# Combined weights' stores issued later, their combination ended earlier, and weight slices loaded ahead in an attention kernel with two expert layers

## The chip, the cores and the metric

The kernel runs on one core of one Trainium2 chip. The metric is the device time of one execution in microseconds. The profile adds one execution with its span (first to last instruction) and a trace of every instruction.

## What is computed

The reference joins an attention between a sequence and a set of states with two feed-forward layers, all in float32:

```python
scores = scale * np.matmul(x, state.transpose(0, 1, 3, 2))   # x: 8 x 8 x 512 x 64, state: 8 x 8 x 32 x 64
a = softmax(scores);        xread = np.matmul(a, state)
scores2 = scale * np.matmul(state, x.transpose(0, 1, 3, 2))
a2 = softmax(scores2);      sread = np.matmul(a2, x)
y = np.concatenate([xread, sread], axis=2)      # -> 4352 tokens x 512
h = y @ w_in                                    # 512 -> 2048, weights moe_*
y = (np.maximum(h, 0.0) + alpha * np.minimum(h, 0.0)) @ w_out
h = y @ w_in2                                   # weights moe2_*
out = (h - np.tanh(h)) @ w_out2
```

## The kernel before

Every float32 matrix is split into a high and a low part of a format that TensorE multiplies fast, and a product is three matmuls (high x high, high x low, low x high). The tokens are worked in nine blocks: blocks 0 to 7 have 512 tokens each (the sequence's reads of one batch), and the states' block has the 256 reads of the states of all batches. The order is 0 to 6, then the states' block, then block 7. In the plan below, index 6 (`B - 2`) is block 6, index 7 (`B - 1`) is the states' block and index 8 (`B`) is block 7.

**First layer.** A block is 16 visits f. Visit f issues the hidden tile f (`emit_h`, line 628), ScalarE and VectorE make the activation g of it (`act_a`, lines 634 and 635; `act_b`, lines 639 and 640), and TensorE adds the output product of the tile two visits back (`emit_o`, line 656), so `emit_o` of the last two tiles of a block falls into the first two visits of the next. In blocks 1 to 7 the weights are projected ones (`pw`), loaded in quarters by `load_parts` (line 443). For the states' block the plain weights are used, a slice of 128 columns per visit (`WS[f]`, tile ws, 512 KB in two DMAs), loaded from a copy in device memory by `load_w_in` (line 459). The block's input is the reads of the states, which each batch's attention stores (`xs<-xw`, line 610) and which are loaded in block 6, visit 13 (`load_reads`, line 699, tile yl). `split_reads` splits them (lines 348 on ScalarE, 349 on VectorE): two of the four column parts in visit 14 of block 6, two in visit 15. Beside this each block prepares the attention of the next ones.

**Combination.** The second layer's weights are used in combined form (a seven-product scheme). The generator `combine` makes them for 2 matrices of 8 pieces. For a piece, two raw tiles (`c_raw`, 512 KB each) are loaded one piece ahead (lines 104 and 110), ScalarE and VectorE turn the 64-bit words into integers (`c_m`, `c_q`, lines 113 to 125), GpSimd adds and subtracts them (`c_q`, `c_s`, line 238 and on), and the inner `parts` makes the split: a ScalarE copy into a `c_o` tile (line 263), GpSimd's subtraction of it (line 265), and the stores to device memory (line 267), seven of 256 KB for a piece. `c_raw` has 4 buffers, `c_o` 3. `combining` runs the second half of one piece step by step with the first half of the next, 9 steps per piece and 144 in all. Before, two steps are taken in each visit from visit 1 of block 3 on, until they are used up.

**Order.** All is written in program order by hand (`tc.manual_schedule`). Work that goes with a visit is put into a plan by `at(block index, visit, place, ...)`, with the places early (after `emit_h`), gap and mid (after `act_a`), late (after `emit_o` and `act_b`) and end. All DMAs are issued by SyncE in that order; an instruction that waits holds up those behind it on its engine. When a tile's buffer is used again, the new writer waits for the last reader of the old tile.

After block 7's third visit `open_slots` frees the combination's tiles (and before, would finish what is left of it), and the second layer begins its loads of combined weights (`ch<-wc`, later `wp<-wc`).

Of the kernel before, what the change touches and what calls it, by code (L numbers as in the profile page):

```python
# [12 lines left out]
F32 = mybir.dt.float32  # L13
F32R = mybir.dt.float32r
# [8 lines left out]
P = 128  # L23
# [12 lines left out]
def attention_and_two_mlps(ctx, tc, x, state, w1_in, w1_out, alpha, w2_in, w2_out, out):  # L36
    nc = tc.nc
    B, H, S, D = x.shape
# [4 lines left out]
    NCC = DM // P  # L43
    NF = DFF // P
# [56 lines left out]
    def raw_words(r, layer, f, half):  # L101
        if half == 0:
            wi = w1_in if layer == 0 else w2_in
            nc.sync.dma_start(
                out=r.rearrange("p (c f) w -> p c (f w)", c=NCC),
                in_=wi[:, 2 * f * P:2 * (f + 1) * P].rearrange("(c p) w -> p c w", p=P),
            )
        else:
            wo = w1_out if layer == 0 else w2_out
            nc.sync.dma_start(out=r.rearrange("p e w -> p (e w)"), in_=wo[f * P:(f + 1) * P, :])  # L110

    def high_abs(m, r):
        nc.scalar.activation(m.bitcast(F32), r[:, :, 1].bitcast(F32), AF.Abs)

    def high_word(m):
        nc.vector.tensor_scalar(m.bitcast(F32), m.bitcast(F32), HIGH_MAX, HIGH_MIN,
                                op0=ALU.min, op1=ALU.max)
        nc.vector.tensor_scalar(m, m, 3, LOW30, op0=ALU.logical_shift_left, op1=ALU.bitwise_and)

    def sign_word(m, r):  # L120
        nc.vector.scalar_tensor_tensor(m, r[:, :, 1], SIGN_TOP, m,  # L121
                                       op0=ALU.bitwise_and, op1=ALU.bitwise_or)

    def low_word(q, r):
        nc.scalar.activation(q, r[:, :, 0].bitcast(U32), AF.Copy, scale=2.0**-29)
# [78 lines left out]
    NJ, HW = NF // 2, DM // 2  # L204
    wc_dram = [[dram.tile([7, 2, P, 2, HW], F32, name=f"wc{m}_{j}") for j in range(NJ // 2)] for m in range(2)]

    def combine(mat, j, take, ahead):

        def raw(m, jj):
            got = []  # L210
            for h in range(2):
                r, done = take("raw")
                raw_words(r, 1, jj + h * NJ, m)
                got.append((r, done))
            return got

        got = ahead.pop((mat, j), None)
        if got is None:
            got = raw(mat, j)
        m, m_done, q, q_done = [], [], [], []  # L220

        def a(h):
            t, done = take("m")
            m.append(t)
            m_done.append(done)
            high_abs(t, got[h][0])

        def b(h):
            high_word(m[h])
            sign_word(m[h], got[h][0])  # L230
            t, done = take("q")
            q.append(t)
            q_done.append(done)
            low_word(t, got[h][0])
            got[h][1]()

        def c(h):
            nc.gpsimd.tensor_tensor(q[h], m[h], q[h], op=ALU.add)  # L238
            m_done[h]()

        a(0)
        yield
        a(1)
        b(0)
        yield
        b(1)
        c(0)
        yield
        c(1)
        n = (mat, j + 1) if j + 1 < NJ else (mat + 1, 0)  # L250
        if n[0] < 2:
            ahead[n] = raw(*n)
        yield "words"
        u, v = (t.bitcast(F32) for t in q)
        s, s_done = take("s")
        one, two = slice(0, HW), slice(HW, DM)
        sub = partial(nc.gpsimd.tensor_tensor, op=ALU.subtract)

        def parts(src, places):
            n = src.shape[-1]  # L260
            o, done = take("o")
            o = o[:, :, :n]
            nc.scalar.copy(o[:, 0], src)  # L263
            yield
            sub(o[:, 1], src, o[:, 0].bitcast(F32))  # L265
            for k, i in enumerate(places):
                nc.sync.dma_start(out=wc_dram[mat][j // 2][i, j % 2], in_=o[:, :, k * HW:(k + 1) * HW].bitcast(F32))
            done()

        if mat == 0:  # L270
            nc.gpsimd.tensor_tensor(s[:, one], v[:, one], v[:, two], op=ALU.add)
            sub(v[:, one], u[:, one], v[:, one])
            yield from parts(u, (0, 5))
            sub(s[:, two], v[:, two], v[:, one])
            yield from parts(v, (4, 6))
            sub(u[:, two], u[:, two], s[:, two])
            yield from parts(s, (1, 2))
            yield from parts(u[:, two], (3,))
        else:
            sub(s[:, one], u[:, one], u[:, two])  # L280
            sub(u[:, one], v[:, one], u[:, one])
            yield from parts(v, (3, 5))
            sub(s[:, two], v[:, one], s[:, one])
            yield from parts(u, (4, 0))
            sub(v[:, two], v[:, two], s[:, two])
            yield from parts(s, (1, 2))
            yield from parts(v[:, two], (6,))
        s_done()
        for done in q_done:
            done()  # L290

    def combining(todo, take):

        ahead, last = {}, None
        for n in [*todo, None]:
            now = combine(*n, take, ahead) if n else None
            working = now is not None
            while working or last is not None:
                if working:
                    working = next(now) != "words"  # L300
                    yield
                if last is not None:
                    if next(last, "end") == "end":
                        last = None
                    yield
            last = now
# [48 lines left out]
    def lead(b):  # L355
        return b if b % 2 else (b - 1) % B
# [95 lines left out]
    WS, late_pools = {}, []  # L452

    def load_w_in(f):
        if f < NF:
            WS[f] = late_pools[0].tile([P, 2, NCC, P], F32R, tag="ws", name=f"ws{f}", bufs=5)
            col = slice(f % FQ * P, (f % FQ + 1) * P)
            for part in range(2):
                nc.sync.dma_start(out=WS[f][:, part].bitcast(F32), in_=wi_dram[f // FQ][part][:, :, col])
# [274 lines left out]
    def load_chunk(o, i):  # L734

        t = slots.get([P, 2, 2, HW], F32R, f"ch{o}_{i}")
        nc.sync.dma_start(out=t.bitcast(F32), in_=wc_dram[0][o][i].rearrange("j p h c -> p j h c"))
        CH[o, i] = t
# [11 lines left out]
    def load_pair(u):  # L750
        for k in range(2):
            for m in range(2):
                load_pair_part(u, k, m)
# [315 lines left out]
    def at(i, f, when, *todo):  # L1069
        plan.setdefault((i, f, when), []).extend(todo)  # L1070
# [28 lines left out]
    with tc.manual_schedule():  # L1099
# [40 lines left out]
        for b in range(2, B):  # L1140
            for g in range(NG):
                i, f = (0, 0) if b == 2 else (b - 2, 6 + 7 * g) if b == lead(b) else (b - 2, 1 + g)
# [48 lines left out]
        def take(what):  # L1191
            shape, dtype, bufs = dict(raw=([P, DM, 2], I32, 4), m=([P, DM], I32, 2), q=([P, DM], I32, 4),
                                      s=([P, DM], F32, 2), o=([P, 2, DM], F32R, 3))[what]
            return late_pools[0].tile(shape, dtype, tag=f"c_{what}", name=f"c_{what}", bufs=bufs), lambda: None

        combined = combining([(m, j) for m in range(2) for j in range(NJ)], take)
        at(3, 0, "late", open_late)
        for i in range(3, B):
            for f in range(1 if i == 3 else 0, NF):
                for when in ("mid", "late"):  # L1200
                    at(i, f, when, lambda: next(combined, None))
        for f in range(4):
            at(B - 2, NF - 4 + f, "late", partial(load_w_in, f))
        for f in range(NF):
            at(B - 1, f, "early", partial(load_w_in, f + 4))

        fill = Filler()

        def open_slots():
            for _ in combined:  # L1210
                pass
            late_pools[0].release()
            freed.append(tc.alloc_tile_pool(name="slots_a", bufs=1, side="right", reuse_waits="tile"))
            slots.add(freed[0], "a", 16)
            load_pair(0)
            for i in range(7):
                load_chunk(0, i)

        freed = []
        at(B, 2, "late", open_slots)  # L1220
        at(B, 6, "early", lambda: fill.start(prepare_pair(0, 0)))
        for f in range(6, NF):
# [7 lines left out]
        for i, f in visits:  # L1230
            blk, n = seq[i]
# [142 lines left out]
```

## Time and profile before

| | |
|---|---|
| median of 3 runs | 1455.9 us (1454.38 to 1461.07) |
| the profiled execution's own time | 1458.23 us |
| its span | 1456.4 us |
| mean granted clock of TensorE | 0.981 of full speed |
| TensorE's busy time | 1393.9 us, 96% of the span |
| VectorE, ScalarE, GpSimd busy | 974.2, 731.0, 536.1 us |

The busy time of TensorE is modelled from its pipelined matmuls, so an engine that is shown busy is not at its peak. A granted clock of 1.00 is 2.4 GHz, 0.5 would be 1.2 GHz, and a value between is a mean over a stretch in which both were granted. An idle time is put down to what ended it.

### The profile page before, as it was taken

The numbers are of one execution on the slowest core, as the hardware profiler recorded it, in microseconds if no ns is written. First come the engines' busy times: TensorE is split into PE (matmuls) and PEld (weight loads), VectorE is DVE, ScalarE is ACT, GpSimd is POOL, SyncE is SP. The second block draws the span as 40 slices with busy tenths as digits, with TensorE's granted clock in tenths as the row PEclk, the third lists the DMA queues.
The fourth block names the chain that finished last, engine by engine and source line by source line (L and its number), as shares of the span: only waits on it lengthen the run. The fifth ranks groups of instructions, "written<-read, shape, count | busy, mean of one in ns | idle before, by whom it ended". The sixth has DMA issues, their size and how long they took to land.

```text
span 1456.4 us, 22830 instructions
## 1 busy us (share of the span) xinstructions
PE 1393.9 (96%) x8142; PEld 1188.7 (82%) x8142; DVE 974.2 (67%) x1436; ACT 731.0 (50%) x1326; POOL 536.1 (37%) x414
## 2 busy tenths in 40 slices
PE   5779899899999999999999999999999999999998
PEld 3557677677777778779977888888879999999998
DVE  7889766556666777764345656565357798877774
ACT  4666554444565656554335545454354354444443
POOL 3645400000554554445002212122035676666652
PEclk8989999999999999999999999999999999999999
DMA  6447568996677777689737774644968733444421
GB/s 184 138 136 210 168 181 313 301 304 192 197 219 216 205 243 221 204 245 307 245 79 273 252 252 153 220 167 146 345 253 319 252 114 120 146 138 138 145 81 37
DMA packets 230946, 293.43 MB, mean 201 GB/s; under 512 B 58288, under 2 KB 134064, under 8 KB 229808
## 3 DMA queue, kind: packets, MB, share of 16 engines
q1 hardware_dynamic: 230832, 291.97, 62.1%
q8 instruction: 64, 1.05, 0.3%
q14 instruction: 50, 0.41, 0.1%
HBM read 169.22 MB, written 120.59 MB: 199 GB/s over the span
## 4 chain that ended last, share of the span: by engine, by line
PE 66%; DVE 9%; DMA 9%; issue 3%; ACT 3%; SPq 2%; POOL 2%; ACTq 0%; DVEq 0%; POOLq 0%
PE ps_m L1038 20%; PE ps_m L848 17%; PE acc L656 15%; PE ps_h L628 9%; PE ps_p L416 2%; DMA wp<-wc 2%; DMA gt<-g 2%; PE ps_m L922 2%; DVE ps_h L635 1%; DVE g L640 1%; DMA pw<-pw 1%; ACT g L639 1%; DMA wc<-c_o 1%; DMA c_raw<-in_moe_w_out 1%; DMA ch<-wc 1%
## 5 line engine op out<-in xcount | busy, mean ns | idle before, releaser
L656 PE MATMUL acc<-g,wo 128*128 128x512 f32 (+1 forms) x1728 | 409.7, 387 | 1.7 <-ACT g L639 1.6
L656 PEld LDWEIGHTS acc<-g,wo 128*128 128x128 f32 x1728 | 315.0, 192 | 73.8 <-issue 6.5
L1038 PE MATMUL ps_m<-wp,s 128*128 128x256 f32 x2856 | 343.4, 283 | 1.1 <-ACT e L1021 1.1
L1038 PEld LDWEIGHTS ps_m<-wp,s 128*128 128x128 f32 x2856 | 343.0, 192 | 1.5 <-ACT e L1021 1.5
L848 PE MATMUL ps_m<-x,ch 128*128 128x512 f32 x1344 | 306.5, 390 | 3.3 <-ACT c L854 2.6
L848 PEld LDWEIGHTS ps_m<-x,ch 128*128 128x128 f32 x1344 | 251.9, 188 | 57.4 <-ACT c L854 3.8
L983 DVE TENSOR_TENSOR s<-gt,s 128x512 fp32r<-128x512 f32 (+1 forms) x216 | 215.2, 1046 | 48.5 <-ACT s L999 47.4
L640 DVE SCALAR_TENSOR_TENSOR g<-ps_h,sign,g 128x512 fp32r<-128x512 f32 (+1 forms) x144 | 103.5, 718 | 158.5 <-ACT g L639 158.4
L639 ACT ACTIVATE g<-ps_h,sign 128x512 fp32r<-128x512 f32 (+1 forms) x144 | 95.6, 664 | 178.5 <-PE acc L656 126.3
L999 ACT CAST s<-gt 128x512 fp32r<-128x512 f32 (+1 forms) x216 | 119.9, 597 | 81.0 <-PE ps_m L1038 38.7
L628 PE MATMUL ps_h<-x,pw 128*128 128x512 f32 x600 | 156.5, 396 | 3.1 <-DVE g L640 1.5
L635 DVE SCALAR_TENSOR_TENSOR ps_h<-ps_h,sign,t 128x512 f32<-128x512 f32 (+1 forms) x144 | 104.4, 725 | 60.2 <-ACT t L634 59.3
L628 PEld LDWEIGHTS ps_h<-x,pw 128*128 128x128 f32 x600 | 109.7, 188 | 28.5 <-DVE g L640 2.1
L861 POOL TENSOR_TENSOR t<-c,t 128x512 f32<-128x512 f32 x32 | 45.2, 1413 | 230.8 <-ACT t L858 225.9
L238 POOL TENSOR_TENSOR c_q<-c_m,c_q 128x512 int32<-128x512 int32 x32 | 41.3, 1292 | 232.7 <-DVE c_m L121 212.9
L870 DVE TENSOR_TENSOR c<-ps_m,c 128x512 f32<-128x512 f32 x96 | 65.8, 689 | 84.4 <-PE ps_m L848 71.8
L634 ACT ACTIVATE t<-ps_h,slope 128x512 f32<-128x512 f32 (+1 forms) x144 | 95.9, 666 | 49.5 <-PE ps_h L628 49.2
L858 ACT ACTIVATE t<-c 128x512 f32<-128x512 f32 x96 | 60.5, 633 | 85.1 <-DVE c L870 75.7
L265 POOL TENSOR_TENSOR c_o<-c_q,c_o 128x512 fp32r<-128x512 f32 (+1 forms) x48 | 56.1, 1169 | 97.0 <-ACT c_o L263 97.0
L965 POOL TENSOR_TENSOR s<-gt,gt 128x512 f32<-128x512 f32 (+1 forms) x36 | 52.8, 1476 | 87.4 <-DMA gt<-g 87.2
L854 ACT COPY c<-ps_m 128x512 f32<-128x512 f32 x96 | 56.0, 587 | 51.7 <-PE ps_m L848 44.6
L168 POOL TENSOR_TENSOR cq<-cm,cq 128x512 int32<-128x512 int32 x32 | 42.6, 1330 | 96.0 <-DVE cm L121 67.0
(146 smaller groups left out, 1647.9 us busy)
## 6 DMA issues: line engine op xcount, KB each, us to landing
g<-t SPq DMA_DIRECT2D x128, 256.0 KB, 2.3
gt<-g SPq DMA_DIRECT2D x64, 512.0 KB, 4.9
wc<-c_o SPq DMA_DIRECT2D x112, 256.0 KB, 3.6
ch<-wc SPq DMA_DIRECT2D x56, 512.0 KB, 7.0
pw<-pw SPq DMA_DIRECT2D x104, 256.0 KB, 5.1
wp<-wc SPq DMA_DIRECT2D x28, 512.0 KB, 7.0
pw<-ph SPq DMA_DIRECT2D x40, 256.0 KB, 2.9
pw<-pl SPq DMA_DIRECT2D x40, 256.0 KB, 2.7
```

Of the source, the lines that this page charges most:

```text
L628: nc.tensor.matmul(ps[:, :n], lhsT=w[i], rhs=xt[:, j, :n], start=(k == 0 and m == 0), stop=(k == len(pairs) - 1 and m == 2))
L634: nc.scalar.mul(t, ph, slope[:, f:f + 1])
L635: nc.vector.scalar_tensor_tensor(ph, ph, sign[:, f:f + 1], t, op0=ALU.mult, op1=ALU.max)
L639: nc.scalar.mul(g[:, 0, :n], ph, sign[:, f:f + 1])
L640: nc.vector.scalar_tensor_tensor(g[:, 1, :n], ph, sign[:, f:f + 1], g[:, 0, :n].bitcast(F32), op0=ALU.mult, op1=ALU.subtract)
L656: nc.tensor.matmul(acc[t][:, :n], lhsT=w[i][:, t * P:(t + 1) * P], rhs=g[:, j, :n], start=(first and k == 0), stop=(last and k == 2))
L848: nc.tensor.matmul(b, lhsT=w[p][:, cc], rhs=XT[key, i][cc][:, q], start=(i not in GOES_ON and cc == k == 0), stop=(cc == 1 and k == 2), sk ...
L858: nc.scalar.activation(t, h, AF.Tanh)
L870: nc.vector.tensor_tensor(h, ps[j, i], h, op=ALU.add)
L983: nc.vector.tensor_tensor(made[k - 1][:, 1], src, made[k - 1][:, 0].bitcast(F32), op=ALU.subtract)
L999: nc.scalar.copy(made[k][:, 0], source(blk, i, jj))
L1038: nc.tensor.matmul(dst[:, t * HW:(t + 1) * HW], lhsT=s[:, p, r, t * P:(t + 1) * P], rhs=w[:, q], start=first, stop=(jj == NJ // 2 - 1 and ...
```

## The change

A store of a combined part is no longer issued where its subtraction is, but kept in a list with the number of the step, and a new `combine_step` issues it after the step whose number is higher by two. In blocks 3 to 6 a third step is taken at the end of every odd visit and of visits 0 and 8; none is planned in the states' block. What would be left at visit 9 of block 6 is done there (`drain`). The slices of the states' block's weights use 12 buffers instead of 5: the 5 of ws, then the 4 of c_raw and the 3 of c_o. Slices 0 to 4 are loaded in visits 2 to 6 of block 6, slices 5 to 11 in visits 9 to 15, and slices 12 to 15 in visits 2 to 5 of the states' block.

```diff
@@ combine, parts @@
             sub(o[:, 1], src, o[:, 0].bitcast(F32))
             for k, i in enumerate(places):
-                nc.sync.dma_start(out=wc_dram[mat][j // 2][i, j % 2], in_=o[:, :, k * HW:(k + 1) * HW].bitcast(F32))
+                kept.append((turns_of[0], wc_dram[mat][j // 2][i, j % 2], o[:, :, k * HW:(k + 1) * HW].bitcast(F32)))
             done()
@@ before combining @@
+    kept, turns_of = deque(), [0]
+
+    def combine_step(n=1):
+        for _ in range(n):
+            turns_of[0] += 1
+            next(combined, None)
+            while kept and kept[0][0] < turns_of[0] - 1:
+                _, o, t = kept.popleft()
+                nc.sync.dma_start(out=o, in_=t)
@@ load_w_in @@
         if f < NF:
-            WS[f] = late_pools[0].tile([P, 2, NCC, P], F32R, tag="ws", name=f"ws{f}", bufs=5)
+            k = f % 12
+            tag, bufs = ("ws", 5) if k < 5 else ("c_raw", 4) if k < 9 else ("c_o", 3)
+            WS[f] = late_pools[0].tile([P, 2, NCC, P], F32R, tag=tag, name=f"ws{f}", bufs=bufs)
@@ the plan @@
         combined = combining([(m, j) for m in range(2) for j in range(NJ)], take)
+        def drain():
+            while next(combined, "end") != "end":
+                pass
+            while kept:
+                _, o, t = kept.popleft()
+                nc.sync.dma_start(out=o, in_=t)
+
         at(3, 0, "late", open_late)
-        for i in range(3, B):
+        for i in range(3, B - 1):
             for f in range(1 if i == 3 else 0, NF):
                 for when in ("mid", "late"):
-                    at(i, f, when, lambda: next(combined, None))
-        for f in range(4):
-            at(B - 2, NF - 4 + f, "late", partial(load_w_in, f))
-        for f in range(NF):
-            at(B - 1, f, "early", partial(load_w_in, f + 4))
+                    at(i, f, when, combine_step)
+                if f % 2 or f % 8 == 0:
+                    at(i, f, "end", combine_step)
+        for f in range(5):
+            at(B - 2, 2 + f, "late", partial(load_w_in, f))
+        at(B - 2, 9, "end", drain)
+        for f in range(5, 12):
+            at(B - 2, 4 + f, "early", partial(load_w_in, f))
+        for f in range(NF - 12):
+            at(B - 1, f + 2, "early", partial(load_w_in, f + 12))
 
         def open_slots():
-            for _ in combined:
-                pass
             late_pools[0].release()
```

## Rows read from the trace of the kernel before

**Rows 1.** The profile page's first line.

```profile
span 1456.4 us, 22830 instructions
```

**Rows 2.** Busy time by stretch: us, busy (instructions) per engine, clock, DMA share, GB/s.

```profile
core 0: us, PE busy (x) PEld busy (x) DVE busy (x) ACT busy (x) POOL busy (x), PEclk, DMA share, GB/s
350.30:645.57 295.27, 292.35 (x1548) 231.14 (x1547) 207.04 (x353) 167.81 (x308) 139.48 (x134) 0.99 0.73 218
645.57:657.20 11.63, 8.06 (x26) 6.03 (x26) 8.22 (x14) 6.13 (x13) 7.71 (x7) 0.71 1.01 297
657.20:678.70 21.50, 21.50 (x171) 21.01 (x170) 13.17 (x22) 12.38 (x26) 13.53 (x15) 1.00 0.96 310
678.70:692.46 13.76, 12.07 (x87) 11.67 (x86) 3.23 (x7) 4.45 (x10) 5.35 (x6) 0.88 0.99 308
692.46:705.25 12.79, 12.79 (x108) 12.79 (x108) 4.40 (x9) 4.28 (x9) 0.00 (x0) 1.00 0.98 246
```

**Rows 3.** The chain of waits, 636 to 712 us: start, us, what.

```profile
640.75 4.17 DMA yl<-xs
...
652.08 5.12 PE acc L656 x12
...
658.68 2.75 PE acc L656 x12
...
692.46 1.44 PE acc L656 x12
```

**Rows 4.** Timeline: first hidden matmuls of the states' block and of block 7.

```profile
645.57 1.15 PE L628 MATMUL ps_h<-x,ws 128*128 128x256 f32 x6
...
705.25 1.55 PE L628 MATMUL ps_h<-x,pw 128*128 128x512 f32 x6
```

**Rows 5.** Timeline of SyncE's DMA issues before the states' block.

```profile
637.37 0.38 SPq L610 DMA_DIRECT2D xs<-xw  x1
637.87 1.18 SPq L267 DMA_DIRECT2D wc<-c_o  x2
639.09 1.33 SPq L459 DMA_DIRECT2D ws<-wi  x2
```

**Rows 6.** Tile yl: who waited for it (us, times).

```profile
  ACT x L348: 5.0, 1
...
  PE ps_h L628: 3.6, 3
```

**Rows 7.** Timeline of ScalarE in the second stall.

```profile
686.62 0.40 ACT L263 CAST c_o<-c_q 128x256 fp32r<-128x256 f32 x1 [2.30 <-DMA wc<-c_o]
686.93 0.47 ACT L639 ACTIVATE g<-ps_h,sign 128x256 fp32r<-128x256 f32 x1
```

**Rows 8.** ScalarE's waits, 345 to 720 us: us in total, times, longest.

```profile
ACT c_m L113 <- DMA c_raw<-in_moe_w_in: 8.3, 3, 3.9
ACT c_o L263 <- DMA wc<-c_o: 6.8, 3, 2.5
```

**Rows 9.** SyncE's queue's waits, 345 to 720 us.

```profile
SPq L267 <- POOL c_o L265: 96.0, 35, 8.4
```

**Rows 10.** Timeline in block 4: a wait of ScalarE, then of TensorE.

```profile
473.46 0.66 ACT L113 ACTIVATE c_m<-c_raw 128x512 f32<-128x512 f32 x1 [3.32 <-DMA c_raw<-in_moe_w_in]
...
485.78 0.65 PE L581 MATMUL ps_r<-xr,e2t 128*32 128x64 f32 x32 [1.87 <-ACT e2t L551]
...
486.37 4.61 PE L656 MATMUL acc<-g,wo 128*128 128x512 f32 x12
```

**Rows 11.** Line 349, a form: ns min/median/max, first and last start.

```profile
L349 DVE TENSOR_TENSOR x<-at,x x14: 679/681/1411, 81.4 to 633.5; 128x512 fp32r<-128x512 f32 x14
```

**Rows 12.** Tile c_raw: its first loads, and the landing of its DMAs.

```profile
L104 SPq DMA_DIRECT2D c_raw<-in_moe_w_in x16: 442/566/628, 350.3 to 491.5; - x16
...
DMA to landing us min/median/max: 3.9/5.6/8.1
```

**Rows 13.** Tile c_o: landing of its stores.

```profile
DMA to landing us min/median/max: 2.4/3.6/8.2
```

## The prediction

> **What bounds the kernel now.** I began with the page's first line for the span [rows 1], then asked for the busy time by stretch around the lines that the diff touches [rows 2]. From the first combining step to the states' block (blocks 3 to 6) TensorE is busy 292.35 of 295.27 us at a granted clock of 0.99. It sets the pace there, and the other engines matter only where they stop it. The states' block is different. Between two stretches with no idle time (657.20 to 678.70 and 692.46 to 705.25) lie one of 11.63 us in which TensorE worked 8.06 at a clock of 0.71, and one of 13.76 us in which it worked 12.07 at 0.88. So the block has two stalls, and after each the engine ran for a while at the lower of its two clock levels (1.2 GHz instead of 2.4).
>
> How much is that? The chain of waits gives undisturbed prices: 1.44 us for 12 matmuls of 256 columns, 2.75 for 12 of 512 [rows 3]. From the block's first hidden matmul at 645.57 to block 7's first at 705.25 [rows 4] 59.7 us pass. The code puts 16 x 12 hidden and 14 x 12 output matmuls of 256 columns there, and two visits' output of block 6, 24 of 512 columns: 360 x 0.12 + 24 x 0.229 = 48.7 us. So 11.0 us are lost. The first stretch holds 1.44 + 2.75 = 4.2 us of work in 11.63, a loss of 7.4, of which 11.63 - 8.06 = 3.6 is idle and the rest lower clock (12 matmuls took 5.12 instead of 2.75 [rows 3]). The second stall has the remaining 3.6.
>
> Next, who caused them. **First stall:** the chain goes through the load of the attention reads (yl<-xs, issued 640.75, 4.17 us [rows 3]). SyncE's timeline shows the order before it [rows 5]: the last reads' store at 637.37, two stores of combined weights at 637.87, a weight slice's two loads at 639.09 that end at 640.42, and only then yl. ScalarE waits 5.0 us for yl, and then TensorE 3.6 us for the split parts [rows 6]. Behind ScalarE's wait stand that visit's activations, and combining work: c_o, c_m and c_q stand between the first and the second pair of yl's casts in program order, as steps of visits 14 and 15. **Second stall:** ScalarE's copy into c_o waits up to 2.5 us, three times, 6.8 together [rows 7, 8], for the store that last read that buffer. Queued behind it is the g activation that TensorE's output matmuls wait for.
>
> In blocks 3 to 6 the waits on SyncE show 96.0 us in 35 waits of a combined store for GpSimd's subtraction [rows 9]: everything issued after it is held up. ScalarE waits there 8.3 us in three waits for raw weights [rows 8]. One of these is followed by a stall of TensorE: c_m 3.32 us late at 473.46, then 1.87 idle at 485.78 and 12 matmuls in 4.61 instead of 2.75 [rows 10]: 3.7 us in all.
>
> **The change part by part.** *Steps.* 16 matrices' pieces x 9 steps = 144. Before: 30 steps in block 3, 32 each in 4 to 6, so 18 are left to the states' block. After: 39 + 42 + 42 = 123, and the last 21 fall into the first eight visits of block 6. The states' block loses all 18: two pieces' ScalarE copies, VectorE words, GpSimd subtractions, 4 raw loads and some 14 stores. Neither c_o's wait nor combining work between yl's casts exists there any more: the second stall goes, -3.6 us.
>
> *yl.* Before it SyncE now has only the reads' store and slice 9's two loads (0.67 us each [rows 5]). Its issue needs the reads' store landed. VectorE and GpSimd no longer combine in visits 8 to 15, and the 1.41 us subtraction [rows 11] falls in visit 11, so the reduction ahead of that store comes earlier too. I estimate 1.3 us (two wc stores) to 4 us sooner. With the same 4.17 us yl lands at 640.9 to 643.6; the block's first half hidden tile is wanted at 645.57, the second about 0.7 us later. Four casts and four subtractions of about 0.4 us, overlapping, fit. -7.4 us if in time; 0 if not.
>
> *Slices.* Twelve slices go into ws, c_raw and c_o buffers in block 6, four follow in the states' block in buffers freed long before. It is 24 DMAs of block 6, 16 us of SyncE issue over 14 visits. Nothing waits for them there but SyncE's queue. With the 18 steps (18/144 of 46 MB, 32 raw loads and 112 stores) and some ten slices moved, blocks 3 to 6 carry 64 + 5.8 + 5.2 = 75 MB, 256 GB/s instead of 218; 310 GB/s were moved at 657 to 679 [rows 2]. Hidden; if not, pw parts come late at visits 4 and 8 of block 6, two stalls, as an estimate at the 3.7 us of [rows 10] each.
>
> *Denser steps.* The first load of raw weights at 350.3 marks visit 1 of block 3 [rows 12], so 63 visits take 295.3 us, 4.69 each. A step came every 2.34 us and comes every 4.69 x 16/42 = 1.79. Total work is the same, rates rise by 1.31. GpSimd's 139.48 of 295.27 us go to about 62%, ScalarE's 167.81 to perhaps 64%, VectorE's 207.04 to 74%: none becomes the bound by its sum, but waits can. *c_o's reuse:* the tightest buffer is subtracted at step 4 of a piece and copied into again at step 8. Four steps were 9.4 us with no such wait; they were 5.8 in the states' block (1.44 each), with three waits; now they are 7.1. *Store two steps later in the program:* in the best case it starts as soon as its subtraction is done, because SyncE runs ahead of the other engines; in the worst it starts two steps before reuse, 3.6 us against a landing of 2.4 to 8.2 (median 3.6) [rows 13]: ScalarE waits 0 to 4.6 us in each of 16 pieces. *Raw loads:* they land after 3.9 to 8.1 us [rows 12] and are wanted three steps on, 5.4 us instead of 7.0; but they are no longer held by the newest subtraction, a gain of two steps, 3.6 us. The bounds for TensorE are: below, the 3.7 us stall goes, -3.7; above, a stall of that size in every second piece, +30. Nearest is the row of c_raw, whose three waits of 8.3 us cost 3.7 [rows 8, 10]; I take half a stall more, +1.9.
>
> A row speaks against denser steps: a VectorE subtraction of 0.68 us took 1.41 at worst, while GpSimd worked [rows 11]. The Trainium skill (SBUF — State Buffer, Who interferes with whom) says a VectorE instruction with two SBUF inputs and a GpSimd one that reads SBUF exclude each other for the whole instruction. By that rule, as an estimate from rows, if all 353 VectorE instructions of blocks 3 to 6 were such, 15% more of them would wait half of some 1.3 us: 34 us more, VectorE at 82%, still no bound, sum unchanged. The trace agrees in that one duration.
>
> **Sum.** -7.4 - 3.6 + 1.9 = -9.1 us. The profiled execution took 1458.23 us around its span of 1456.4, so 1449.1; it lies 2.3 over the median of 1455.9, so the median becomes 1446.8. I count under 0.5% (7.3 us) as no change.
>
> **Rivals.** *Denser combining stops TensorE (slower).* Place: ScalarE's c_o or c_m wait in blocks 3 to 6, price 3.7 us each. For: 7.1 us lies between the spacing that waits and the one that doesn't. Against: only one of three raw waits reached TensorE. Two to four more give -11.0 + 7.4 to 14.8, 1452.3 to 1459.7; from five on (11.0 + 7.3 = 18.3 us) it is slower, 1463.4 and up.
> *yl stays late.* For: slice loads are now in front of it too. Against: two stores fewer, a freer ScalarE. Gain 3.6 - 1.9 = 1.7: 1454.2.
> *Blocks 3 to 6 gain as well.* The 96.0 us of SyncE's waits end and raw weights come in time: -11.0 - 3.7 = -14.7: 1441.2.
>
> **Chances.** Forecast 0.50 (own range 1444 to 1450); yl late 0.12; some denser stalls 0.14; five or more 0.12; blocks 3 to 6 gain 0.12. Faster: 0.44 of the forecast and the last, 0.56. Slower 0.12. Same: the rest, 0.32. The range 1441 to 1457 leaves out the slow case and a little of its neighbour.
>
> **What would show it.** In the states' block no c_o, no wait of ScalarE for yl above 1 to 2 us, TensorE idle below 1 us from its first to its last hidden tile, clock 1.00, and a length near 49 us instead of 59.7. In blocks 3 to 6 SyncE's waits for GpSimd at the stores nearly gone, c_o and c_m waits of ScalarE under 15 us, TensorE idle of 2 to 5 us. Wrong if the idle time there passes 10 us, or if ScalarE still waits 4 us for yl. Everything behind block 7 should shift as a whole, since what waits there waits for TensorE or for loads issued after it.

## The result and the profile after

The changed kernel takes 1470.89 us (median of 4 runs, 1467.58 to 1472.94) against 1457.91 (4 runs): a ratio of 1.0089, 95% interval 1.0070 to 1.0107. It is slower, by 13 us, where 9 us less were forecast. Its profiled execution took 1472.94 us with a span of 1471.1, 14.7 more than [rows 1].

Busy time by stretch of the changed kernel, cut at the first combining load (349.4), the first hidden matmul of the states' block (670.40) and the first of block 7 (719.07); columns as in [rows 2]:

```profile
349.40:670.40 321.00, 299.98 (x1549) 231.97 (x1547) 229.91 (x370) 179.59 (x330) 169.16 (x160) 0.98 0.80 238
670.40:719.07 48.67, 48.67 (x385) 47.69 (x384) 17.19 (x34) 16.59 (x34) 0.00 (x0) 1.00 0.42 109
719.07:1471.10 752.03, 741.21 (x4706) 674.47 (x4704) 488.35 (x584) 347.21 (x616) 281.56 (x184) 1.00 0.52 183
```

The second line answers to the four lines of [rows 2] from 645.57 to 705.25. The states' block has no idle time left and its clock is 1.00: 48.67 us instead of 59.7, the 11.0 us that were forecast. The first line answers to the first of [rows 2]: blocks 3 to 6 take 321.0 us instead of 295.3, and TensorE is idle for 21.0 of them instead of 2.9. The other 7.6 of the 25.7 us are a longer busy time of the same matmuls (299.98 instead of 292.35). As an estimate from the granted clocks of 20 us windows, at most 3.4 of these are the lower clock level: the two windows below lose 3.4 and 1.8 us by their mean clocks of 0.83 and 0.91, and before one window lost 1.8 (480 to 500, 0.91).

```profile
460.00:480.00 20.00, 16.85 (x96) 12.87 (x95) 15.82 (x29) 11.19 (x22) 12.00 (x12) 0.83 0.56 158
...
560.00:580.00 20.00, 15.87 (x64) 12.38 (x63) 11.02 (x18) 10.62 (x21) 10.48 (x10) 0.91 0.78 252
```

What follows block 7's start takes 752.0 us, before 751.15 (1456.4 - 705.25). So -11.0 + 25.7 and some small change at both ends (-0.9 and +0.9) make the 14.7.

The load of the reads did come early. Tile yl: its issue, and who waited for it:

```profile
L711 SPq DMA_DIRECT2D yl<-xs x2: 402/510/619, 661.6 to 662.3; - x2
...
  ACT x L358: 1.0, 1
```

It is issued 8.8 us before the block's first hidden matmul (before: 4.8, [rows 3, 4]), and ScalarE waits 1.0 us where it waited 5.0 [rows 6].

The new idle time lies in front of attention's matmuls and of output matmuls. TensorE's waits and ScalarE's waits for DMAs, 345 to 740 us (us in total, times, longest):

```profile
PE ps_e L561 <- ACT e L543: 7.5, 3, 3.3
PE ps_st L379 <- DVE sm L371: 4.9, 3, 1.8
PE acc L668 <- DVE g L652: 3.3, 5, 1.3
```

```profile
ACT c_o L263 <- DMA wc<-c_o: 23.9, 13, 4.9
...
ACT c_m L113 <- DMA c_raw<-in_moe_w_out: 3.5, 1, 3.5
...
ACT c_m L113 <- DMA c_raw<-in_moe_w_in: 0.4, 1, 0.4
```

The waits for raw weights fell from 9.9 us (the 8.3 of [rows 8] and 1.6 at the second matrix) to 3.9 (the two lines on c_m); those for a c_o buffer rose from 6.8 [rows 8] to 23.9. SyncE's waits in the same stretch:

```profile
SPq L622 <- DVE xw L621: 54.1, 9, 8.7
SPq L300 <- POOL c_o L265: 53.3, 24, 5.1
```

The 96.0 us of [rows 9] fell to 53.3, but the wait of the reads' store (xs<-xw) for VectorE's reduction grew to 54.1 from 32.8. Three views of one place show how these hang together. SyncE's issues in block 3, ScalarE's and VectorE's instructions:

```profile
385.23 0.57 SPq L300 DMA_DIRECT2D wc<-c_o  x1
389.91 0.37 SPq L622 DMA_DIRECT2D xs<-xw  x1
390.38 2.89 SPq L453 DMA_DIRECT2D pw<-pw  x4
393.37 1.22 SPq L300 DMA_DIRECT2D wc<-c_o  x2
```

```profile
398.55 0.41 ACT L263 CAST c_o<-c_q 128x256 fp32r<-128x256 f32 x1 [3.77 <-DMA wc<-c_o]
```

```profile
389.61 0.28 DVE L621 TENSOR_REDUCE xw<-ps_w 128x64 f32<-128x128 f32 x1
389.80 0.94 DVE L116 TENSOR_SCALAR c_m<-c_m 128x512 f32<-128x512 f32 x1
390.78 1.41 DVE L118 TENSOR_SCALAR c_m<-c_m 128x512 int32<-128x512 int32 x1
392.22 1.11 DVE L121 SCALAR_TENSOR_TENSOR c_m<-c_raw,c_m 128x512 int32<-128x512 int32 x1
393.25 0.75 DVE L647 SCALAR_TENSOR_TENSOR ps_h<-ps_h,sign,t 128x512 f32<-128x512 f32 x1
```

From 385.8 to 389.9 SyncE stands at the reads' store, behind it four loads of parts, and only at 393.37 and later the combined stores that ScalarE's next copies need: ScalarE is held up for 3.77 us. And VectorE's three word instructions take 0.94, 1.41 and 1.11 us, 3.5 in all, before it makes the activation; the same three took 0.41, 0.43 and 0.69 some two us earlier.

### The profile page after: what moved, and what is told of

Read it like the earlier page. It is cut to its first block, busy times and chain, and to the rows that moved or that the text cites. A ratio compares the mean times of both kernels' runs of the same rounds, so it can differ in the third digit from the quotient of the medians.

```text
span 1471.1 us, 22841 instructions
## 1 busy us (share of the span) xinstructions
PE 1394.1 (95%) x8142; PEld 1183.7 (80%) x8142; DVE 988.5 (67%) x1436; ACT 732.4 (50%) x1326; POOL 537.6 (37%) x414
## 4 chain that ended last, share of the span: by engine, by line
PE 66%; DVE 11%; DMA 8%; ACT 4%; issue 3%; SPq 2%; POOL 2%; ACTq 0%; DVEq 0%; POOLq 0%
PE ps_m L1050 20%; PE ps_m L860 18%; PE acc L668 14%; PE ps_h L640 8%; DMA wc<-c_o 2%; PE ps_p L426 2%; DVE ps_h L647 2%; DMA gt<-g 2%; PE ps_m L934 2%; DVE g L652 1%; ACT g L651 1%; DVE c_m L118 1%; DVE c_m L121 1%; DMA wp<-wc 1%; DMA pw<-pw 1%
## 5 line engine op out<-in xcount | busy, mean ns | idle before, releaser
L995 DVE TENSOR_TENSOR s<-gt,s 128x512 fp32r<-128x512 f32 (+1 forms) x216 | 218.3, 1061 | 46.8 <-ACT s L1011 45.8
L781 POOL TENSOR_TENSOR rx<-rx,rx 128x1024 f32<-128x1024 f32 x8 | 19.5, 2440 | 172.2 <-DMA pw<-pw 106.5
```

Source lines behind the costliest of these rows:

```text
L995: nc.vector.tensor_tensor(made[k - 1][:, 1], src, made[k - 1][:, 0].bitcast(F32), op=ALU.subtract)
```

## The experiments

The theories after the result: **A**, ScalarE's wait for c_o's buffers, caused by stores that stand later in SyncE's queue; **B**, the denser steps as such, whatever the stores do. The measure is the stretch from each run's own first combining load to the first hidden matmul of the states' block (295.3 us before, 321.0 after), beside the block itself (59.7 and 48.7). How much one profile can tell is seen in the code that no edit touches: in the eleven profiles the first combining load comes at 349.4 to 352.6 us, and what follows block 7's start takes 750.0 to 753.8. So a difference of 3 or 4 us between the stretches of two kernels counts as shown only where their medians show it too.

**Stores at once.** The changed kernel with

```diff
-            while kept and kept[0][0] < turns_of[0] - 1:
+            while kept and kept[0][0] <= turns_of[0]:
```

> The changed kernel, but each combined store is issued right behind the step of its subtraction (no lag of two steps); density, three c_o buffers and preloaded slices stay. Theory A (c_o's reuse: in the changed kernel ScalarE waits 23.9 us in 13 waits for stores that stand two steps later in SyncE's queue, behind the reads' store and the parts' loads): c_o waits fall below 10 us, the stretch from the first combining load to the states' block falls from 320 us to 300 to 310, total 1452 to 1461. Theory B (density: a third step per odd visit overfills VectorE and ScalarE whatever the stores do): c_o waits may fall, the stretch stays above 314, total 1465 or more.

Measured: 1461.31 us, ratio 1.0030 (1.0018 to 1.0042) to the kernel before; the stretch 312.0, the block 48.7, c_o waits 5.0 us. So with three buffers 9.0 of the 25.7 us come from the lag. Waits for raw weights rise to 14.4 us. The rest stays: the stretch lies between the ranges of both theories, and A explains a part.

**Four c_o buffers, lag kept.**

```diff
-            tag, bufs = ("ws", 5) if k < 5 else ("c_raw", 4) if k < 9 else ("c_o", 3)
+            tag, bufs = ("ws", 4) if k < 4 else ("c_raw", 4) if k < 8 else ("c_o", 4)
...
-                                      s=([P, DM], F32, 2), o=([P, 2, DM], F32R, 3))[what]
+                                      s=([P, DM], F32, 2), o=([P, 2, DM], F32R, 4))[what]
...
-        for f in range(5):
+        for f in range(4):
             at(B - 2, 2 + f, "late", partial(load_w_in, f))
...
-        for f in range(5, 12):
+        for f in range(4, 12):
```

> The changed kernel with four c_o buffers and four ws buffers in the same space (slices 0 to 3 in ws, 4 to 7 in c_raw, 8 to 11 in c_o); the lag of two steps stays. Theory A (the wait for the buffer makes the loss): c_o waits under 5 us, the stretch 298 to 306 us, total 1448 to 1457. Theory B (density): c_o waits under 5 us too, but the stretch stays above 314 us, total 1465 or more.

Measured: 1459.20 us, ratio 1.0013 (1.0000 to 1.0026); the stretch 308.3, c_o waits 1.7 us, raw waits 7.4. With the buffer's wait gone 12.7 us come back, and 13.0 us over the kernel before remain. Neither theory's numbers hold; both have a share.

**Both edits.**

> The changed kernel with both: no lag and four c_o buffers. Theory A: c_o waits 0 to 2 us, the stretch 296 to 303 us, total 1446 to 1453, no better than the four buffers alone by more than 4 us. Theory B: the stretch above 312 us, total 1463 or more. If lag costs something beyond the buffer, this is clearly faster than the four buffers with lag.

Measured: 1462.78 us, ratio 1.0034 (1.0021 to 1.0047); the stretch 311.0, no c_o wait, raw waits 11.1. So 15.7 us of loss have nothing to do with c_o. With four buffers the lag does no harm and perhaps some good: 308.3 with it, 311.0 without, beside 7.4 against 11.1 us of waits for raw weights; the medians lie 3.6 us apart, with intervals that just overlap.

**The lag alone.** The kernel before, with `kept` and `combine_step` in the two places of a visit that it has.

> The kernel before with only the stores' lag of two steps; steps, buffers and slices stay where they were. If the lag alone harms through c_o's reuse: c_o waits well above the 6.8 us of before (15 us or more, most in the states' block where steps are 1.44 us apart), total 1460 or more. If the lag harms only together with denser steps: blocks 3 to 6 stay at 293 to 298 us, waits for raw weights fall below 9.9 us, and only the states' block grows by 0 to 4 us, total 1455 to 1461.

Measured: 1462.06 us, ratio 1.0036 (1.0022 to 1.0050). c_o waits 23.9 us in 12 waits, half of it (12.1) in blocks 3 to 6 where there was none; the reads' store holds SyncE for 63.6 us, the stretch takes 298.7 (to 651.25, where TensorE begins to wait) and the states' block 63.7. The lag is no gain in itself: with three buffers it costs at the old density too. By the medians that is 5.7 us (1462.06 against 1456.40 in the same set of runs); in the profiled execution, which at 1466.71 us was the longest of its nine, it is 3.4 us in blocks 3 to 6 and 4.0 in the states' block.

**A milder density.** The kernel before, with the 18 steps of the states' block moved into blocks 3 to 6:

```diff
-        for i in range(3, B):
+        for i in range(3, B - 1):
             for f in range(1 if i == 3 else 0, NF):
-                for when in ("mid", "late"):
+                for when in ("mid", "late") + (("end",) if f % 4 == 2 or (f == 8 and i > 4) else ()):
```

> The kernel before with one thing changed: the combining steps that fell into the states' block are spread over blocks 3 to 6 as a third step in 18 of the 63 visits, ending with block 6; stores at once, three c_o buffers, slices loaded as before. Both theories: the states' block loses its second stall (3.6 us) and, if the combining work among yl's casts made the first stall and not the slice load in front of yl, most of that too (7.4 us). Theory A: 2.06 us a step instead of 1.79 leaves c_o nearly free of waits, total 1446 to 1452. Theory B: half of the density's cost remains, 1454 to 1462.

Measured: 1456.85 us, ratio 0.9994 (0.9980 to 1.0008): no change. The stretch 299.1 (+3.8), the block 54.2 (-5.5). The second stall is gone. The first is not: ScalarE waits 5.0 us for yl as before. SyncE's issues there:

```profile
643.36 0.38 SPq L610 DMA_DIRECT2D xs<-xw  x1
643.79 1.25 SPq L459 DMA_DIRECT2D ws<-wi  x2
645.08 1.13 SPq L699 DMA_DIRECT2D yl<-xs  x2
```

The last reads' store comes 7.5 us before the block's first hidden matmul (650.85); before it was 8.2 ([rows 4, 5]) and in the changed kernel 10.5. It waits for VectorE's reduction, which ends at 643.33; VectorE has combining words here up to block 6's last visits. Behind the store stands a slice's load. The load of yl is issued 5.8 us ahead, which is 1.0 more than before, but takes 5.3 us to land instead of 4.3, so nothing is won. Combining between yl's casts and before the store, and the slice, were not told apart here; the last kernel below removes all three.

**Which engine do the denser steps overfill?** Three kernels on top of the one with four buffers and lag (308.3). They leave work out, so their weights are not the reference's, and only their times count. First, two of the three word instructions of VectorE left out (lines 116 and 118, both in `high_word`):

```diff
-            high_word(m[h])
             sign_word(m[h], got[h][0])
```

> The changed kernel with four c_o buffers, which leaves out two of the three VectorE instructions that make an integer word (the clamp and the shift, lines 116 and 118; about 47 us of VectorE in blocks 3 to 6), so the weights are not the reference's. Theory VectorE (the remaining 14 us over the stretch of before come from VectorE being late where combining meets attention): the stretch falls from 309 to 294 to 300 us, total 1443 to 1450. Theory GpSimd or ScalarE: it stays above 304 us, total 1454 or more.

Measured: 1448.72 us, ratio 0.9948 (0.9928 to 0.9968); the stretch 297.0, VectorE's busy time down by 41 us:

```profile
352.10:649.07 296.97, 293.17 (x1548) 230.85 (x1547) 188.91 (x306) 180.22 (x330) 171.64 (x160) 0.99 0.86 258
```

ScalarE and GpSimd do as much as before this cut, in less time, and DMA is at its densest (0.86): none of them is the limit. Second, GpSimd's additions left out:

```diff
-            nc.gpsimd.tensor_tensor(q[h], m[h], q[h], op=ALU.add)
             m_done[h]()
```

> The changed kernel with four c_o buffers, which leaves out GpSimd's addition of the two word parts (line 238, 41 us of GpSimd), so the weights are not the reference's; VectorE's instructions all stay. Theory VectorE's own work: VectorE's busy time falls only by what the collisions with GpSimd cost it (5 to 10 us), the stretch stays at 303 us or more. Theory collisions or GpSimd's lateness: the stretch falls to 294 to 300 us as without the words.

Measured: 1465.60 us, ratio 1.0058 (1.0038 to 1.0077); the stretch 312.7, with GpSimd busy 131.1 instead of 168.3 and VectorE 231.2 instead of 230.2. GpSimd's amount of work is not what holds TensorE up. Why the stretch is 4 us longer than with the additions stays open; the three word lines (116, 118, 121) take 73.7 us in all there, 70.4 with the additions. Third, the sums left out instead:

```diff
-            nc.gpsimd.tensor_tensor(s[:, one], v[:, one], v[:, two], op=ALU.add)
-            sub(v[:, one], u[:, one], v[:, one])
             yield from parts(u, (0, 5))
-            sub(s[:, two], v[:, two], v[:, one])
             yield from parts(v, (4, 6))
-            sub(u[:, two], u[:, two], s[:, two])
-            yield from parts(s, (1, 2))
+            yield from parts(u, (1, 2))
...
```

> The changed kernel with four c_o buffers, which leaves out GpSimd's ten additions and subtractions that form the sums of a pair of matrices' pieces (lines 271 to 285; some 54 us of GpSimd), so the weights are not the reference's; GpSimd's word additions and the subtractions of the split stay, VectorE's instructions all stay. Without the word additions the stretch stayed at 312.7 us. Theory VectorE's own work at the higher rate: the stretch stays at 304 us or more and line 118 keeps a median near 0.85 us. Theory collisions with GpSimd's two-input work stretch VectorE: line 118's median falls to 0.43, VectorE's busy time in the stretch from 230 to 220 us or less, the stretch falls to 295 to 301 us.

Measured: 1457.87 us, ratio 1.0007 (0.9993 to 1.0022); the stretch 304.8, VectorE busy 218.8 instead of 230.2. Line 118 with the sums (four buffers), and without them (ns, min/median/max):

```profile
L118 DVE TENSOR_SCALAR c_m<-c_m x32: 426/846/1420, 361.6 to 612.2; 128x512 int32<-128x512 int32 x32
```

```profile
L118 DVE TENSOR_SCALAR c_m<-c_m x32: 426/427/1422, 362.1 to 609.5; 128x512 int32<-128x512 int32 x32
```

So denser steps let the words fall onto GpSimd's sums, which doubles line 118's usual time; before, its median was 428 ns. What this costs the kernel is small and not clear of noise: the stretch is 3.5 us shorter without the sums, but the medians' ratios (1.0007 and 1.0013) differ by less than their intervals.

The kernel without the sums doesn't take all collisions away, though: in each of the last two kernels GpSimd's subtractions of the split (line 265 of the changed kernel) remain, and the words fall onto these too. An estimate from the traces: in the stretch of the kernel with four buffers VectorE's instructions together take 32.6 us more than if each took the shortest time of its kind (differences above 0.1 us each). All of this excess lies beside GpSimd instructions, 15.8 us beside line 265, 13.4 beside the sums, 3.4 beside the additions. It was 18.2 us before, and is 20.9 without the sums. So it is the words that hold TensorE up (11.3 of the 13.0 us go with two of their instructions), but how much of that is VectorE's own work at the higher rate, and how much its collisions with line 265, isn't shown. The timeline of the kernel with four buffers shows the manner:

```profile
556.03 1.29 POOL L238 TENSOR_TENSOR c_q<-c_m,c_q 128x512 int32<-128x512 int32 x1 [1.15 <-ACT c_q L125]
...
556.47 1.14 DVE L116 TENSOR_SCALAR c_m<-c_m 128x512 f32<-128x512 f32 x1
...
557.29 1.47 POOL L265 TENSOR_TENSOR c_o<-c_q,c_o 128x512 fp32r<-128x512 f32 x1
557.65 1.39 DVE L118 TENSOR_SCALAR c_m<-c_m 128x512 int32<-128x512 int32 x1
...
559.07 1.11 DVE L121 SCALAR_TENSOR_TENSOR c_m<-c_raw,c_m 128x512 int32<-128x512 int32 x1
560.11 0.75 DVE L647 SCALAR_TENSOR_TENSOR ps_h<-ps_h,sign,t 128x512 f32<-128x512 f32 x1
...
562.08 0.15 DVE L539 TENSOR_SCALAR nb<-mx 128x1 f32<-128x1 f32 x1
562.27 0.69 ACT L543 ACTIVATE e<-ps_s,nb 128x512 f32<-128x512 f32 x1 [5.72 <-DVE nb L539]
...
563.10 1.12 PE L561 MATMUL ps_e<-ident,e 128*128 128x128 f32 x4 [2.29 <-ACT e L543]
```

Three word instructions of 3.6 us together, beside an addition and a subtraction of GpSimd, stand before the softmax's maximum (alone they take 1.5); ScalarE waits 5.72 us for it, and TensorE 2.29 us for ScalarE's exponentials. Two windows of the same kernel show VectorE nearly full where its mean over the stretch is 230.15 of 308.34 us, 75%; the third line is the fullest such window of the kernel before:

```profile
380.00:400.00 20.00, 19.65 (x89) 15.14 (x89) 17.71 (x28) 11.71 (x22) 15.62 (x15) 1.00 0.57 164
...
460.00:480.00 20.00, 16.95 (x79) 12.43 (x78) 17.72 (x28) 11.23 (x22) 13.67 (x13) 1.00 0.76 207
```

```profile
600.00:620.00 20.00, 20.00 (x122) 15.38 (x120) 16.96 (x31) 10.91 (x20) 9.96 (x10) 1.00 0.39 123
```

A full window alone doesn't stop TensorE: it was busy for 19.65 us in the first of the three and for all 20.00 in the last.

**A version that keeps the gain without the density.** The kernel before, with

```diff
-        for i in range(3, B):
-            for f in range(1 if i == 3 else 0, NF):
-                for when in ("mid", "late"):
+        for i in range(3, B - 1):
+            for f in range(1 if i == 3 else 0, NF if i < B - 2 else NF - 3):
+                for when in ("mid", "late") + (("end",) if f in (3, 11, 15) else ()):
                     at(i, f, when, lambda: next(combined, None))
-        for f in range(4):
-            at(B - 2, NF - 4 + f, "late", partial(load_w_in, f))
-        for f in range(NF):
-            at(B - 1, f, "early", partial(load_w_in, f + 4))
+        for f in range(2, 15):
+            at(B - 1, f, "late", lambda: next(combined, None))
+        for f in range(5):
+            at(B - 2, 7 + f, "late", partial(load_w_in, f))
+        for f in range(NF - 5):
+            at(B - 1, f + 1, "early", partial(load_w_in, f + 5))
```

> The kernel before, rearranged: stores at once, three c_o buffers; no combining step in visits 13 to 15 of block 6; 11 third steps in blocks 3 to 6; the last 13 steps one in a visit of the states' block (2.9 us apart); slices 0 to 4 loaded in visits 7 to 11 of block 6, the others five ahead, so that none stands in front of yl. By the forecast's reading of the states' block both stalls go (length 49 to 52 us instead of 59.7); by the measured price of density (5.3 us for 18 third steps) blocks 3 to 6 grow by 3 us. Total 1446 to 1452, faster than both kernels. If a step in the states' block still stalls it, 1453 or more.

Measured: 1449.15 us, ratio 0.9945 (0.9929 to 0.9962), faster than both kernels. Its stretch (296.0), with 11 third steps, and its states' block (to 695.95):

```profile
351.30:647.28 295.98, 291.57 (x1548) 229.85 (x1547) 215.95 (x364) 173.80 (x319) 150.58 (x144) 1.00 0.79 234
647.28:695.95 48.67, 48.67 (x385) 47.68 (x384) 19.92 (x40) 21.81 (x45) 16.06 (x16) 1.00 0.79 244
```

No c_o wait, 0.6 us of wait for yl, and 13 combining steps in a states' block of 48.67 us without an idle moment: neither an empty block nor 12 preloaded slices are needed for its 11 us. Of the 10.3 us that the two stretches give, 7.6 are left in the span, because the untouched code took 1.0 us longer ahead of them and 1.7 behind them in this execution.

## Why the prediction was wrong

**What held.** The reading of the states' block: two stalls, 11.0 us, from c_o's wait there and from the late yl. The block shrank by 11.0 us to 48.67, against 48.7 worked out from rows. The 1.3 to 4 us that I gave to yl's earlier issue came out as 4.0 (8.8 against 4.8 us ahead). DMA traffic was hidden, as said: 238 GB/s in blocks 3 to 6, and no wait of TensorE for parts there. Everything behind block 7 shifted as a whole, within 0.9 us.

**The step that failed** is "Denser steps", sized +1.9 us between bounds of -3.7 and +30. It measured +25.7, and the sign named for being wrong, 10 us of idle TensorE, came with 21.0. Two parts of it failed, each for its own reason.

*The later store* (12.7 us, the part that a fourth buffer gives back). I had let the store start "as soon as its subtraction is done, because SyncE runs ahead of the other engines", and had named the other end, two steps before reuse. SyncE runs ahead only as far as the next store that has to wait. Its queue holds in each block two reads' stores that wait for VectorE, and it stood at them for 32.8 us before, for 54.1 in the changed kernel and for 63.6 with the lag alone (with four buffers, 49.4 with the lag and 29.7 without). In the lag a store is moved past these and past the loads of parts; that is what the move cost, and I had not gone through the queue to see it. I had seen that ScalarE may wait "0 to 4.6 us in each of 16 pieces" for the buffer, but the sum put this at nothing, without a reason; it waited 23.9 us in 13 waits, of up to 4.9. The lag alone, at the old spacing of 9.4 us, brought 12.1 us of c_o waits into blocks 3 to 6; closer steps without the lag brought 5.0. Together they brought 23.9.

*The rate* (13.0 us, measured with four buffers and the lag). I priced it by ScalarE's waits for raw weights and the one stall of [rows 10], and judged the engines by their means: 74% for VectorE "none becomes the bound by its sum, but waits can". The raw waits in fact fell. The place was VectorE, which is in the middle of TensorE's chains (activation, maximum, reads' reduction). Without two of its word instructions 11.3 of the 13.0 us come back. The row that I priced from pointed there too: between the late c_m at 473.46 and TensorE's idle time at 485.78 ScalarE waits for VectorE:

```profile
483.53 0.63 ACT L544 ACTIVATE sc<-sc 128x512 f32<-128x512 f32 x1 [3.04 <-DVE sc L542]
```

The collisions with GpSimd, which I had weighed by a rule and left at no cost, were real. VectorE's busy time in the stretch rose from 207.0 us before to 229.9 in the changed kernel. The three word lines make 19.4 us of this: four more word tiles (32 instead of 28) are some 6, and the remaining 13 are slower words. The rule was that of the Trainium skill (SBUF — State Buffer, Who interferes with whom). I had taken from it what it says of instructions with two inputs in SBUF, while line 118 has one; the same section counts `tensor_scalar`, which line 118 is, among those that can enter a two-port mode and then contend with GpSimd, under conditions on their operands. The trace agrees in kind, with line 118's median of 428 ns before and 845 after, but no run shows which mode it was in. How the 13.0 us divide between VectorE's longer queue and its slower words stays open, since leaving words out takes both away, and leaving the sums out takes only some of the collisions.

**The rivals.** "Denser combining stops TensorE" is the one that came, and its threshold (18.3 us) was passed. Its place was right for the c_o half only, and its chance of 0.12 for the slower case was too small: the sum had an upper bound of +30 in sight, and two unpriced changes (rate and lag) pointed the same way. "Blocks 3 to 6 gain as well" fell, although the waits on SyncE that it rested on did shrink from 96.0 to 53.3 us: they had not been what TensorE waited for. (Those 96.0 us were also not all of blocks 3 to 6: the row runs from 345 to 720 us, and 86.7 of them lie in these blocks.) "yl stays late" didn't come: ScalarE waited 1.0 us for it.

## What to carry to other kernels

Before a store is moved later in an in-order queue, read what it is moved past; if something there waits for another engine, the buffer that the store frees is late by that wait, and here a spare buffer was worth more than a freer queue. When filler work is packed closer, its price may lie not in the mean load of the engines but in the latency of the one that stands in the middle of the chains: follow a wait of the bound engine back to what stood in front of it there. And a stage that stalls because of filler work need not be emptied of it: thinning it to one step a visit, and clearing the way of the one late load, gave the whole gain here at almost no loss.

## What was not expected of the hardware

A VectorE instruction on integers (128x512, line 118) took one of three times, by what GpSimd did beside it. In the kernel with four buffers 11 of its 32 had no GpSimd instruction beside them and took 0.43 us, 16 lay beside a sum of 128x256 and took 0.83 to 0.85, and 5 lay beside an addition or subtraction of 128x512 and took 1.4. The kernel before has the slowest case as its usual one early in the run, where the same line works on other tiles:

```profile
L118 DVE TENSOR_SCALAR cm<-cm x32: 426/1380/1527, 18.6 to 176.9; 128x512 int32<-128x512 int32 x32
```

And 32 GpSimd additions of 128x512 left out of the stretch changed neither VectorE's busy time (231.2 against 230.2 us) nor the stretch for the better: here it was not the amount of GpSimd's work that slowed VectorE, but which of it fell together with VectorE's words.
